# k^T v of a linear-attention block: the last 64 positions as products of 64 rows, and another written-out order of the steps

## The chip, the cores and the metric

The kernel runs on one core of a Trainium2 chip. The metric is the device time of one execution, in microseconds (us); the median of several executions is compared. [...]

## The reference

Eight batches, eight heads, 576 positions, head size 64. What must be computed, for each batch:

```python
q_s = softmax(q, over the head's 64 channels)
k_s = softmax(k, over the 576 positions)
x   = q_s @ (k_s^T @ v)                  # per head, heads side by side: (576, 512)
h   = gelu(x @ w_in)                     # (576, 1024); u, v = halves of 512 columns
v_n = layer_norm(v) * g_ln
out = x + (u * (w_sg @ v_n + b_sg)) @ w_out
```

The results are wanted in float32. The large products are made from float32 numbers that are split in a high and a low part (three products for one); the products of the attention are taken in plain float32, and each of those shows as two matmul instructions in the trace.

## The kernel before

Everything is written out: `PLAN` is a text of 1199 steps such as `hu_mm 3 1`, each a function with its arguments (batch first), and the kernel calls them in that order. Each engine issues its own instructions in that order (`InOrder`, and `keep_in_program_order` for matmuls); the letters V, A and G at the end of a step put it on VectorE (DVE), ScalarE (ACT) or GpSimd (POOL). All transfers are issued by SyncE, in the order of the plan too.

The steps of one batch `b`: `load_k`, `load_v`, `load_q` for each half `h` of the heads (four heads in a half); `k_sub`, `k_exp` (softmax of k without its sum; the column maxima come through `load_kt`, `kt_max`, `kt_put`, `kt_get`); `kv_mm b h`, which makes k^T v and, by a column of ones in v, the sums; `kv_inv` and `kv_scale` divide; `q_max` to `q_mul` make the softmax of q and `q_turn` transposes it; `x_mm b h` makes x; `x_high` and `x_low` split it. Then the block of the MLP: `hv_mm b i` (v half, with `hv_gelu`, `hv_stat`, `hv_pow`, `hv_norm`, `hv_high`, `hv_low`), `hu_mm b f` (u half, with `hu_gelu`), `sg_mm`, `gate`, `gate_high`, `gate_low`, `out_mm`, `out_add`, `out_rest`, `out_store`. Four pieces of 128 columns make one matrix; positions are 4 x 128 and a rest of 64, and the rests of two batches share one `hv_mm b 4`.

Sums lie in PSUM: `ps2` has three buffers of two banks (for `x`, `hu_mm`, `sg_mm`, `out_mm`), `ps1` two buffers of one bank (`kv_mm`, `hv_mm`), each taken in turn.

Batch 0 and the weights are the start. `load_q0` to `q0_copy` prepare q of batch 0, `k0_max`, `k0_mm`, `k0_exp`, `k0_less`, `k0_copy` its k, which is turned on TensorE (`k0_mm b p both` also adds the negated maxima by a second product). `load_w_in f`, `wi_a`, `wi_b`, `wi_d` rebuild a float32 piece of w_in from words in three passes (ACT, DVE, DVE), `wi_h` makes the high part and `wi_l` the low part; pieces 4 and 6 are pairs of 256 columns, so of twice the size. Pieces 0 to 3 are for `hu0_mm f j s` (batch 0's u half, in parts), 4 to 7 for `hv_mm`. Before any data has come, `busy(ps1[0], 21)` issues 21 products of ones, which are not used.

Before, `kv_mm b h` puts the products of one half of the heads in one bank. The fifth block of 128 rows holds the last 64 positions; its other 64 rows of v are zeros.

Of the kernel before, what the change touches and what calls it, by code (L numbers as in the profile page):

```python
# [38 lines left out]
kv_mm 0 1, load_w_in 1, load_w_in 2, q0_turn 0 0, q0_copy 0 1, wi_a 1, wi_b 3, wi_d 3, kv_inv 0 1, q0_copy 0 0, k0_mm 0 0, load_v 0 0, q0_mul 1 1
q0_turn 1 1, k0_mm 0 1, k0_copy 0 0, wi_b 1, load_w_in 0, kv_scale 0 1, wi_a 2, k0_copy 0 1, x0_mm 1 0, wi_h 3 G, q0_copy 1 1, wi_d 1, wi_h 1 G  # L40
kv_mm 0 0, wi_l 3 V, wi_b 2, x0_high 1 0, wi_d 2, neg, load_q 1 0, wi_l 1 V, x0_mm 1 1, kv_inv 0 0, wi_a 0, kv_scale 0 0, load_q 1 1, x0_high 1 1
wi_h 2 G, q_max 1 0, load_w_in 6, x0_neg 1 0, x0_mm 0 0, x0_low 1 0 A, x0_high 0 0, q_max 1 1, x0_neg 1 1, wi_l 2, x0_low 1 1 A, load_w_in 7
# [4 lines left out]
hu0_mm 2 0 0, hu0_mm 1 0 0, hu0_gelu 1 1, hu0_mm 2 1 0, hu0_gelu 2 0, load_w_out 1, hu0_gelu 2 1, hu0_mm 3 0 0, hu0_gelu 3 0, hv_mm 0 3, load_w_out 0
k0_max 1 2, q_sum 1 0, load_kt 2 0, q_swapd 1 0 G, hu0_gelu 1 0, hv_mm 0 0, k0_less 1 1, load_w_sg 0, q_sum 1 1, k0_less 1 0, q_swapd 1 1 G, k0_mm 1 0
k0_less 1 3, k0_less 1 2, q_inv 1 0, q_mul 1 0 1, q_mul 1 0 0, q_inv 1 1, q_turn 1 1, q_mul 1 1 1, k0_mm 1 1, k0_mm 1 2, hv_gelu 0 3, q_turn 1 0
k0_copy 1 1, wo_a 2, wo_b 2, hv_gelu 0 0 A, k0_copy 1 0, hv_mm 0 2, hv_gelu 0 2 A, q_turn 1 3, k0_mm 1 3, k0_copy 1 2, k0_copy 1 3, load_w_sg 1  # L50
kv_mm 1 0, kv_inv 1 0, kv_scale 1 0, wo_a 0, wo_d 2, load_kt 2 1, kv_mm 1 1, kv_inv 1 1, x_mm 1 0, wo_b 0, wo_d 0, hv_sq 0 0, kv_scale 1 1
hu0_mm 0 0 1, hu0_mm 0 0 0, q_mul 1 1 0, q_turn 1 2, load_w_sg 3, hv_mm 0 1, ws_h 0, ws_l 0, load_w_sg 2, x_high 1 0, x_low 1 0, x_high 1 1, x_low 1 1
x_mm 1 1, hv_sq 0 2, hv_gelu 0 1, hv_stat 0 3, hu0_mm 0 1 1, hv_norm 0 3, hv_norm 0 0, hv_stat 0 0 A, hv_pow 0 0, load_v 2 0, hv_stat 0 2 A
x_high 1 3, load_w_sg 4, x_high 1 2, hv_pow 0 2, x_low 1 2, hu0_mm 0 1 0, x_low 1 3, hv_high 0 0, hv_low 0 0, hv_pow 0 3, hv_high 0 3, hv_norm 0 2
hv_low 0 3, kt_max 2 1, load_q 2 0, kt_max 2 0, ws_h 2, ws_l 2 V, hv_stat 0 1, hv_norm 0 1, hv_high 0 2, hv_mm 0 4, hv_gelu 0 4 A, hv_sq 0 4
hv_pow 0 1, hv_mm 1 2, hv_gelu 1 2 A, hv_low 0 2, ws_h 4, load_b, load_v 2 1, hv_stat 0 4 A, hv_pow 0 4, wo_h 2, hv_mm 1 3, b_h, hv_gelu 1 3
hv_high 0 1, q_max 2 0, hv_norm 0 4, wo_h 0 V, load_kt 2 3, kt_max 2 3, load_kt 2 2, hv_mm 1 1, kt_max 2 2, hv_low 0 1, hv_mm 1 0, load_q 2 1
tail_high 0, tail_again 0, ws_l 4 V, hu0_gelu 0 0, tail_high 1, load_k 2 0, hu0_gelu 0 1, q_swapm 2 0 G, hv_stat 1 3, tail_low 0, b_l, sg_mm 0 0
hv_gelu 1 1 A, hv_sq 1 1, hv_norm 1 1, gate 0 0, load_kt 3 0, gate_high 0 0, q_max 2 1, q_swapm 2 1, hv_pow 1 3, sg_mm 0 1, kt_put 2, kt_get 2
load_k 2 1, wo_l 2 V, hv_sq 1 2, gate_low 0 0, gate 0 1, kt_max 3 0, gate_high 0 1, sg_mm 0 2, gate 0 2, gate_high 0 2, wo_l 0, sg_mm 0 3  # L60
tail_again 1, gate_low 0 1, k_sub 2 0, gate_low 0 2 G, gate 0 3, gate_high 0 3, gate_low 0 3, k_sub 2 1, out_mm 0 2, tail_low 1, k_exp 2 0, k_exp 2 1
q_top 2 0, q_sub 2 0 V, out_mm 0 1, hv_stat 1 1 A, q_top 2 1, q_sub 2 1 V, hv_norm 1 3, out_add 0 2, out_add 0 1, q_exp 2 1, q_exp 2 0, load_kt 3 1
q_sum 2 0, hv_gelu 1 0 A, hv_sq 1 0, hv_stat 1 2 A, hu_mm 1 0, q_sum 2 1, hv_pow 1 2, hv_norm 1 2, hv_high 1 2, q_swapd 2 1 G, kt_max 3 1
hv_stat 1 0 A, q_swapd 2 0 G, q_inv 2 0, q_mul 2 0 0, load_kt 3 3, q_turn 2 0, hv_pow 1 0, out_mm 0 3, hu_gelu 1 0, out_add 0 3, hv_norm 1 0
q_mul 2 0 1, out_rest 0 2 V, hu_mm 1 2, hv_high 1 0, hv_low 1 0, kt_max 3 3, out_mm 0 0, hv_pow 1 1, kv_mm 2 0, load_k 3 0, kv_mm 2 1, hv_high 1 3
kv_inv 2 0, hu_gelu 1 2, out_add 0 0, hu_mm 1 3, hu_gelu 1 3, q_turn 2 1, load_q 3 0, out_rest 0 0 V, kv_scale 2 0, kv_inv 2 1, kv_scale 2 1
hv_low 1 2, hv_high 1 1, hv_low 1 1, q_inv 2 1, q_mul 2 1 1 V, load_kt 3 2, q_turn 2 3, hv_low 1 3, q_mul 2 1 0 V, q_max 3 0, q_swapm 3 0 G, hu_mm 1 1
kt_max 3 2, sg_mm 1 0, q_top 3 0, q_turn 2 2, gate 1 0, q_sub 3 0, hu_gelu 1 1, sg_mm 1 1, gate 1 1, gate_high 1 1, sg_mm 1 2, gate 1 2, x_mm 2 0
gate_high 1 0, gate_low 1 0 G, x_high 2 1, out_rest 0 1 V, out_rest 0 3, x_high 2 0, x_low 2 1, gate_low 1 1, gate_high 1 2, sg_mm 1 3, x_low 2 0
gate 1 3, q_exp 3 0, gate_high 1 3, x_mm 2 1, q_sum 3 0, q_swapd 3 0, x_high 2 2, x_high 2 3, gate_low 1 2 G, gate_low 1 3, q_inv 3 0, x_low 2 2  # L70
x_low 2 3, load_q 3 1, q_mul 3 0 1, out_store 0 2, out_mm 1 2, out_add 1 2, q_max 3 1, hv_mm 2 0, load_k 3 1, hv_gelu 2 0, hv_stat 2 0, hv_norm 2 0
q_swapm 3 1, q_top 3 1, q_sub 3 1 V, q_exp 3 1, hv_pow 2 0, hv_high 2 0, q_sum 3 1, out_mm 1 1, hv_mm 2 1, hv_gelu 2 1 A, out_store 0 1, q_mul 3 0 0
kt_put 3, kt_get 3, k_sub 3 1, out_mm 1 3, k_sub 3 0, q_swapd 3 1 G, out_add 1 1, out_rest 1 1 V, q_inv 3 1, out_store 0 0, q_mul 3 1 1 V, out_mm 1 0
out_add 1 0, hv_sq 2 1, load_v 3 1, load_v 3 0, q_turn 3 1, out_rest 1 0, hu_mm 2 2, q_turn 3 0, k_exp 3 0, kv_mm 3 0, out_store 0 3, out_add 1 3
out_rest 1 3 V, kv_inv 3 0, kv_scale 3 0, k_exp 3 1, kv_mm 3 1, q_mul 3 1 0, kv_inv 3 1, x_mm 3 0, out_rest 1 2 V, load_kt 4 0, hv_stat 2 1 A
load_v 4 0, x_high 3 1, hv_mm 2 2, x_high 3 0, out_store 1 1, q_turn 3 2, kv_scale 3 1, hu_gelu 2 2, x_low 3 1, q_turn 3 3, hv_norm 2 1, x_low 3 0
hv_low 2 0, hv_mm 2 3, x_mm 3 1, hv_gelu 2 3 A, hv_sq 2 3, hu_mm 2 0, hv_gelu 2 2 A, x_high 3 2, x_low 3 2, x_high 3 3, x_low 3 3, load_q 4 1
out_store 1 0, out_store 1 3, hv_mm 2 4, hv_sq 2 2, hv_stat 2 2 A, hv_gelu 2 4, hv_stat 2 3 A, q_max 4 1, q_swapm 4 1 G, kt_max 4 0, hu_gelu 2 0
# [843 lines left out]
```

## Time and profile before

| | |
|---|---|
| median of 3 executions | 496.68 us (495.06 to 497.91) |
| the profiled execution, its own time | 495.04 us |
| its span, first to last instruction | 493.3 us |
| TensorE busy in the span | 486.4 us (99%) |
| VectorE, ScalarE, GpSimd busy | 336.3, 239.0, 153.1 us |

A row of the trace gives the start in us from the span's start, the duration, the engine, the line of the code (a helper's, here always L241 for matmuls and L154 for the other engines), the operation, and what it writes and reads by the names of the tiles. Matmuls overlap in the array, so the distance between two starts tells more than one duration does.

### The profile page before, as it was taken

The page shows a single profiled execution, that of the slowest core. Times are in us where ns is not written, and L with a number is a line of the kernel's source. Part 1 is how long each engine was busy: PE and PEld are TensorE (multiplying, and loading weights), DVE is VectorE, ACT ScalarE, POOL GpSimd, SP SyncE. Part 2 cuts the span into 40 slices and gives each one's busy share as a digit, 9 for nine tenths or more (in the row PEclk, how much of TensorE's full clock was granted, in tenths as well). Part 3 has the DMA queues.
Part 4 walks back from the last instruction along what each step waited for, and adds up shares of the span by engine and source line. Part 5 has one row for each costly group of instructions (what it writes and reads, how often), then busy time and mean ns, then how long its engine had stood idle before and what let it go on. Part 6 is the DMA issues. An engine that isn't in the chain of part 4 may idle for free.

```text
span 493.3 us, 9408 instructions
## 1 busy us (share of the span) xinstructions
PE 486.4 (99%) x3881; PEld 448.3 (91%) x3881; DVE 336.3 (68%) x550; ACT 239.0 (48%) x402; POOL 153.1 (31%) x189
## 2 busy tenths in 40 slices
PE   7999999999999999999999999999999999999997
...
DVE  7998997877679576787575577785659753353232
...
PEclk9999999999999999999999999999999999999999
...
GB/s 306 360 389 246 176 175 76 25 79 101 182 143 78 206 125 88 49 177 251 2 155 22 63 219 47 25 102 154 45 256 25 24 76 0 1 0 2 96 1 96
DMA packets 20637, 57.28 MB, mean 116 GB/s; under 512 B 3057, under 2 KB 3569, under 8 KB 20594
## 3 DMA queue, kind: packets, MB, share of 16 engines
...
## 4 chain that ended last, share of the span: by engine, by line
PE 94%; DVE 3%; DMA 2%; issue 1%; ACT 0%; SPq 0%
PE ps L241 94%; DMA qq<-q 2%; DVE o L154 1%; DVE wi_l L154 1%; DVE qd L154 0%; DVE k0m L154 0%; ACT o L154 0%; DVE qm L154 0%; DVE qq L154 0%; SPq L154 0%
## 5 line engine op out<-in xcount | busy, mean ns | idle before, releaser
L241 PE MATMUL ps<-ulow,wo_h 128*128 128x288 f32 (+1 forms) x260 | 56.6, 295 | 0.0
L241 PE MATMUL ps<-gh,wo_h 128*128 128x288 f32 (+1 forms) x260 | 56.5, 295 | 0.0
L241 PE MATMUL ps<-gh,wo_l 128*128 128x288 f32 (+1 forms) x260 | 56.4, 294 | 0.0
L154 DVE TENSOR_TENSOR u<-ps,u 128x576 f32<-128x576 f32 x32 | 23.9, 754 | 46.1 <-PE ps L241 45.9
L241 PE MATMUL ps<-ws_h,vnh 128*128 128x288 f32 x256 | 55.1, 296 | 0.0
L241 PE MATMUL ps<-ws_l,vnh 128*128 128x288 f32 x256 | 54.8, 295 | 0.0
L241 PE MATMUL ps<-ws_h,vnl 128*128 128x288 f32 x256 | 54.8, 295 | 0.0
L154 POOL TENSOR_TENSOR rs<-ve,half 128x1 f32<-128x1 f32 x36 | 26.8, 752 | 90.1 <-DVE ve L154 90.0
L154 ACT CAST gh<-u 128x576 fp32r<-128x576 f32 x32 | 21.1, 670 | 58.2 <-DVE u L154 58.2
L154 ACT ACT_TABLE_LOAD x32 | 41.1, 1283 | 14.5 <-issue 3.5
L154 ACT ACTIVATE u<-ps 128x576 f32<-128x576 f32 (+2 forms) x36 | 21.0, 596 | 50.6 <-PE ps L241 42.1
L241 PE MATMUL ps<-x_h,wi_h 128*128 128x288 f32 (+2 forms) x256 | 42.4, 300 | 1.0 <-ACT u L154 1.0
L241 PEld LDWEIGHTS ps<-gh,wo_h 128*128 128x128 f32 x260 | 42.2, 188 | 0.8 <-issue 0.4
L241 PEld LDWEIGHTS ps<-ws_h,vnh 128*128 128x128 f32 x256 | 41.6, 188 | 1.4 <-DVE u L154 0.9
L154 POOL TENSOR_TENSOR ulow<-u,gh 128x576 fp32r<-128x576 f32 x15 | 24.0, 1598 | 60.5 <-ACT gh L154 50.7
L241 PEld LDWEIGHTS ps<-gh,wo_l 128*128 128x128 f32 x260 | 42.2, 188 | 0.0
L241 PEld LDWEIGHTS ps<-ulow,wo_h 128*128 128x128 f32 x260 | 42.0, 188 | 0.1
L241 PEld LDWEIGHTS ps<-x_h,wi_h 128*128 128x128 f32 x256 | 36.5, 188 | 5.4 <-issue 2.6
L241 PEld LDWEIGHTS ps<-ws_h,vnl 128*128 128x128 f32 x256 | 41.3, 188 | 0.0
L241 PEld LDWEIGHTS ps<-ws_l,vnh 128*128 128x128 f32 x256 | 41.3, 188 | 0.0
L241 PE MATMUL ps<-x_h,wi_l 128*128 128x288 f32 (+2 forms) x256 | 41.3, 296 | 0.0
L241 PE MATMUL ps<-x_l,wi_h 128*128 128x288 f32 (+2 forms) x256 | 41.2, 295 | 0.0
...
## 6 DMA issues: line engine op xcount, KB each, us to landing
...
```

The lines of the kernel that those rows point to most:

```text
L154: ins = op(*args, **kw)
L241: tc.keep_in_program_order(nc.tensor.matmul(*args, **kw))
```

## The change

The new kernel has `kv_all b` in place of the two `kv_mm b h` for batches 2 to 7. It makes the four full blocks of rows for both halves of the heads first, and then the last 64 positions as products of 64 rows: head pair `a = 0` uses the upper 64 rows of the array and of the data, `a = 1` the lower ones, so v now holds the last positions in both halves of its fifth block. The sums of `a` lie in the bank of `a`, with both `h` in it, which turns the places in `kvt` (`kv_of`). Batches 0 and 1 keep `kv_mm`.

`k0_mm 0 3` is the first product with data (before, `k0_mm 0 2`) and gets four more products of ones after its first transposition.

The order of nearly all steps is another one, and many steps change engine: the high parts of w_in go from POOL to DVE (`wi_h` 1, 0, 6) and ACT (2, 3, 4), four of the low parts from DVE to POOL (`wi_l` 1, 0, 3, 4) and `wi_l 2` from POOL to DVE; `q0_sub 1 1` and `k0_copy 0 0` go to DVE; six of twelve `k_sub` go from DVE to POOL. No step other than `kv_mm` and `kv_all` is added or removed.

```diff
     def k0_mm(b, p, both=0, n=0):
         ps, t = flat(bank(ps2, "k0", b, p)), kt0(b, p)
-        busy(ps[:, 0:DV], n)
         for i in range(5):
             c = min(i * P, S - P)
             mm(ps[:, i * P:i * P + P], t[:, c:c + P], eye, is_transpose=True, start=True, stop=not both)
+            busy(ps1[0], n * (i == 0))
+    def kv_all(b):
+        for a in range(2):
+            bank(ps1, "kv", b, a)
+        pk = [sums(st["kv", b, a]) for a in range(2)]
+        for h in range(2):
+            for a in range(2):
+                for i in range(4):
+                    for z in range(2):
+                        c = a * P + z * D
+                        mm(pk[a][z * D:z * D + D, h, :], kk_s(b, h)[:, i, c:c + D], vv_s(b, h)[:, i, 2 * a + z, :], start=h == i == 0, stop=False, skip_group_check=h == 1)
+        for h in range(2):
+            for a in range(2):
+                for z in range(2):
+                    c, rs = a * P + z * D, slice(a * TL, a * TL + TL)
+                    mm(pk[a][z * D:z * D + D, h, :], kk_s(b, h)[rs, 4, c:c + D], vv_s(b, h)[rs, 4, 2 * a + z, :], start=False, stop=True, skip_group_check=h == 1)
+    def kv_of(b, h, a):
+        return kvt_s(b, a)[:, h] if b > 1 else kvt_s(b, h)[:, a]
# in x_mm:      kvt_s(b, h)[zs, a]  ->  kv_of(b, h, a)[zs]
# in kernel():
-    vs[:2, S:] = vs[:2, ST * P:S]
+    vs[:, S:] = vs[:, ST * P:S]
# PLAN before, in part:
-load_q0 1 0, q0_max 1 0, q0_sub 1 0, load_q0 0 1, q0_max 0 1, load_q0 1 1, q0_exp 1 0, q0_max 1 1, q0_sum 1 0, q0_sub 0 1, q0_sub 1 1, load_k0 0 3
-load_k0 0 2, q0_exp 0 1, q0_exp 1 1, q0_sum 0 1, q0_inv 1 0, q0_inv 0 1, k0_max 0 2, load_eye, k0_mm 0 2 1, load_q0 0 0, q0_max 0 0, q0_mul 0 1
...
-load_w_out 2, q_exp 1 0, load_k0 1 3, load_k0 1 0, wi_l 0 V, wi_a 4, wi_d 6, hu0_mm 1 0 1, hu0_mm 1 1 1, q_exp 1 1, hu0_mm 1 1 0, wi_h 6 G, load_v 1 1
-wi_b 4, wi_d 4, wi_h 4 G, load_g, k0_max 1 1, hu0_mm 3 1 0, hu0_gelu 3 1, wi_l 6 V, load_w_out 3, wi_l 4 V, k0_max 1 3, k0_max 1 0, load_v 1 0
# PLAN after, in part:
+load_q0 0 0, q0_max 0 0, q0_sub 0 0, q0_exp 0 0, load_q0 1 1, q0_max 1 1, load_q0 1 0, q0_sub 1 1 V, q0_exp 1 1, q0_max 1 0, q0_sub 1 0, q0_sum 1 1
+load_q0 0 1, q0_max 0 1, q0_exp 1 0, load_k0 0 3, load_eye, q0_inv 1 1, q0_sub 0 1, load_k0 0 2, load_w_in 2, q0_exp 0 1, k0_max 0 3, k0_mm 0 3 1 4
...
+kv_mm 0 0, load_w_in 6, wi_l 0, wi_l 3, x0_neg 1 0, x0_neg 1 1, kv_inv 0 0, kv_scale 0 0, x0_low 1 0 A, q_max 1 0, x0_mm 0 0, x0_low 1 1 A, x0_mm 0 1
+x0_high 0 0, x0_neg 0 0, load_w_in 7, q_max 1 1, x0_high 0 1, q_swapm 1 0 G, x0_low 0 0 A, load_w_in 4, x0_neg 0 1, q_top 1 0, q_sub 1 0 V
+x0_low 0 1 A, load_w_in 5, load_k0 1 1, load_w_out 1, q_swapm 1 1, hu0_mm 2 0 1, hu0_mm 2 1 1, hu0_mm 2 0 0, hu0_mm 2 1 0, q_top 1 1, wi_a 6
+load_k0 1 2, hu0_mm 3 0 1, hu0_mm 3 1 1, load_k0 1 0, hu0_mm 1 0 1, q_exp 1 0, q_sub 1 1 V, q_exp 1 1, load_k0 1 3, hu0_mm 3 1 0, load_w_out 0, wi_b 6
+hu0_mm 1 1 1, wi_d 6, load_w_out 3, wi_h 6 V, hu0_mm 1 1 0, hu0_mm 1 0 0, wi_a 4, wi_b 4, hu0_gelu 2 1, hu0_gelu 3 1, wi_d 4, hu0_mm 3 0 0, wi_l 6 V
+load_v 1 1, wi_h 4, wi_l 4, hu0_gelu 2 0, load_v 1 0, k0_max 1 2, hu0_gelu 1 1, hu0_gelu 3 0, q_sum 1 1, hv_mm 0 3, load_w_out 2, k0_max 1 3
...
+q_turn 3 0, q_turn 3 1, out_mm 1 2, out_add 1 2, hu_mm 2 2, hu_gelu 2 2, kv_all 3, kt_max 4 1, q_mul 3 1 1, hu_mm 2 3, q_turn 3 3, kv_inv 3 0
+load_kt 4 3, out_rest 1 2, out_rest 1 3, hu_gelu 2 3, load_v 4 0, kv_scale 3 0, kv_inv 3 1, kv_scale 3 1, load_q 4 0, x_mm 3 0, hv_stat 2 3 A
...
+gate_low 7 3, out_mm 7 0, out_add 7 0, out_store 7 0, out_mm 7 1, out_add 7 1, out_store 7 1, out_mm 7 2, out_add 7 2, last_mm 7 0, both 7 3 V
+out_store 7 2, last_mm 7 2, last_add 7 0, last_add 7 2, last_store 7 0, last_store 7 2, last_mm 7 1, last_add 7 1, last_store 7 1
```

On TensorE, by the plans, the neighbours of these steps change as follows. Before, in batches 3, 5, 6 and 7 the two `kv_mm` are followed directly by `x_mm b 0`; in batches 2 and 4 another product lies between. After, another product (`hu_mm` or `out_mm`) follows `kv_all` in all six. `x_mm b 0` and `x_mm b 1` stand apart in all batches, before and after. In batch 0 the small products stood as three groups (`x0_mm 1 0, kv_mm 0 0, x0_mm 1 1`, then `x0_mm 0 0`, then `x0_mm 0 1`) and stand as two (`x0_mm 1 0, x0_mm 1 1, kv_mm 0 0`, then `x0_mm 0 0, x0_mm 0 1`).

## Rows read from the trace of the kernel before

**Rows 1.** The page: busy time of each engine (share of the span, instructions), and the span in 40 slices with the granted TensorE clock and the DMA engines' share, in tenths.

```profile
PE 486.4 (99%) x3881; PEld 448.3 (91%) x3881; DVE 336.3 (68%) x550; ACT 239.0 (48%) x402; POOL 153.1 (31%) x189
...
PE   7999999999999999999999999999999999999997
...
DVE  7998997877679576787575577785659753353232
...
PEclk9999999999999999999999999999999999999999
```

**Rows 2.** The chain of work that ended last, in order of time (start, us, what); the parts from the first product with data to the end.

```profile
9.49 8.56 PE ps L241 x94
...
18.11 4.91 DMA qq<-q
...
32.94 1.23 DVE o L154
34.17 0.66 DVE k0m L154
34.83 2.67 DVE wi_l L154 x2
37.54 118.88 PE ps L241 x1008
...
156.46 334.02 PE ps L241 x2592
```

**Rows 3.** What TensorE's matmuls waited for in the whole span (us in total, times, longest).

```profile
PE ps L241 <- POOL vn L154: 1.3, 1, 1.3
PE ps L241 <- DVE k0m L154: 1.1, 1, 1.1
PE ps L241 <- ACT u L154: 1.0, 1, 1.0
```

**Rows 4.** The order of time on TensorE around small products (start, duration, x count), in the start and in batches 2 and 3.

```profile
18.66 0.66 PE L241 MATMUL ps<-qt,kvt 64*64 64x256 f32 x8
19.26 1.39 PE L241 MATMUL ps<-vv,kk 128*64 128x65 f32 x40
20.57 0.77 PE L241 MATMUL ps<-qt,kvt 64*64 64x320 f32 x8
21.27 0.50 PE L241 MATMUL ps<-x_h,minus 128*128 128x256 f32 x2
...
105.09 0.43 PE L241 MATMUL ps<-ulow,wo_h 128*128 128x288 f32 x2
105.35 0.43 PE L241 MATMUL ps<-gh,wo_l 128*128 128x288 f32 x2
105.71 2.55 PE L241 MATMUL ps<-vv,kk 128*64 128x65 f32 x80
108.19 0.80 PE L241 MATMUL ps<-x_h,wi_h 128*128 128x288 f32 x4
...
125.98 1.20 PE L241 MATMUL ps<-qt,kvt 64*64 64x288 f32 x16
127.11 0.53 PE L241 MATMUL ps<-ws_h,vnh 128*128 128x288 f32 x2
```

**Rows 5.** Busy time of the engines in one stretch of the start (us; stretch, its length, then PE, PEld, DVE, ACT, POOL, granted clock, DMA share, GB/s).

```profile
3.40:32.00 28.60, 27.13 (x256) 22.30 (x256) 26.10 (x48) 22.32 (x36) 14.13 (x17) 1.00 1.00 374
```

**Rows 6.** The order of time on TensorE at the end of the start: the last `hu0_mm`, and `hv_mm 0 3` (rows of `wi_h,x_h`, `wi_h,x_l`, `wi_l,x_h`).

```profile
32.73 0.46 PE L241 MATMUL ps<-x_l,wi_h 128*128 128x320 f32 x2
34.19 0.50 PE L241 MATMUL ps<-x_h,wi_h 128*128 128x256 f32 x2 [1.01 <-ACT u L154]
...
34.77 0.40 PE L241 MATMUL ps<-x_l,wi_h 128*128 128x256 f32 x2
35.33 1.21 PE L241 MATMUL ps<-wi_h,x_h 128*128 128x512 f32 x4 [0.17 <-POOL wi_h L154]
36.38 1.09 PE L241 MATMUL ps<-wi_h,x_l 128*128 128x512 f32 x4
37.54 1.20 PE L241 MATMUL ps<-wi_l,x_h 128*128 128x512 f32 x4
```

**Rows 7.** Groups of instructions by operation and shape (busy us in all, mean ns of one): the steps that change engine, and their nearest kin on the engine they go to.

```profile
L154 DVE TENSOR_TENSOR wi_l<-o,wi_h 128x512 fp32r<-128x512 f32 x3 | 2.0, 682 | 0.0
L154 DVE CAST wo_h<-o 128x1024 fp32r<-128x1024 f32 x1 | 0.7, 685 | 0.0
L154 DVE TENSOR_TENSOR qq<-qq,qd 128x512 f32<-128x512 f32 x1 | 0.7, 693 | 0.0
L154 DVE TENSOR_TENSOR o<-ps,o 128x576 f32<-128x576 f32 x3 | 2.3, 758 | 5.8 <-PE ps L241 5.8
...
L154 POOL CAST wi_h<-o 128x1024 fp32r<-128x1024 f32 x2 | 2.1, 1046 | 5.5 <-DVE o L154 5.5
L154 POOL TENSOR_TENSOR wo_l<-o,wo_h 128x1024 fp32r<-128x1024 f32 x1 | 2.7, 2661 | 0.0
...
L154 ACT CAST wo_h<-o 128x1024 fp32r<-128x1024 f32 x1 | 1.1, 1053 | 0.0
```

**Rows 8.** The order of time on VectorE in the start (start, duration; in brackets the idle time before it and what ended it).

```profile
4.44 0.82 DVE L154 TENSOR_REDUCE qm<-qq 128x10 f32<-128x640 f32 x1 [0.27 <-DMA qq<-q]
6.03 0.82 DVE L154 TENSOR_REDUCE qm<-qq 128x10 f32<-128x640 f32 x1 [0.77 <-DMA qq<-q]
...
8.74 0.69 DVE L154 TENSOR_REDUCE k0m<-ukt 128x1 f32<-128x576 f32 x1
...
20.69 0.16 DVE L154 TENSOR_SCALAR kr<-ps 128x2 f32<-128x2 f32 x1 [0.26 <-PE ps L241]
...
23.04 1.35 DVE L154 TENSOR_REDUCE qm<-qq 128x36 f32<-128x1152 f32 x1 [0.41 <-DMA qq<-q]
```

**Rows 9.** Groups as in rows 7: what VectorE and POOL have between `kv_all 3` and `x_mm 3 0` in the new order.

```profile
L154 DVE STREAM_TRANSPOSE qt<-qq 128x576 f32<-128x576 f32 x28 | 21.1, 766 | 4.5 <-POOL qq L154 4.4
...
L154 DVE TENSOR_TENSOR kvt<-ps,kr 128x128 f32<-128x128 f32 x16 | 4.6, 285 | 0.3
...
L154 DVE RECIPROCAL kr<-kr 128x2 f32<-128x2 f32 x16 | 2.7, 166 | 0.5
...
L154 POOL TENSOR_TENSOR qq<-qq,qd 128x576 f32<-128x576 f32 x19 | 24.4, 1294 | 7.4 <-ACT x_h L154 3.8 <-DVE qd L154 2.6 <-DVE qm L154 0.9
```

**Rows 10.** The order of time on VectorE at the end of the span: the last `last_add`.

```profile
490.51 0.31 DVE L154 TENSOR_TENSOR o<-ps,o 128x144 f32<-128x144 f32 x1 [0.84 <-PE ps L241]
```

More of the change, by code (lines that the diff above doesn't have):

```diff
@@ L39 @@
[L39 to L42, printed above, removed]
@@ L47 @@
[L47 to L50, printed above, removed]
@@ L51 @@
[L51 to L78, printed above, removed]
@@ L99 @@
-out_add 3 2, load_kt 6 1, out_rest 3 2, out_add 3 1, q_mul 5 1 1, kv_inv 5 0, hv_stat 4 0 A, kv_scale 5 0, q_mul 5 1 0, q_turn 5 2, hv_norm 4 0
-kv_mm 5 1, kv_inv 5 1, out_rest 3 1 V, out_store 3 1, x_mm 5 0, x_high 5 0, hv_high 4 3, out_store 3 0, hv_mm 4 2, x_high 5 1, x_low 5 1, kv_scale 5 1
-hv_gelu 4 2 A, hv_low 4 3, hv_sq 4 2, hv_pow 4 0, q_turn 5 3, load_q 6 1, x_low 5 0, hu_mm 4 1, load_k 6 0, x_mm 5 1, hu_gelu 4 1, x_high 5 2
-x_low 5 2, kt_max 6 2, hv_high 4 0, hu_mm 4 3, load_k 6 1, q_max 6 1, x_high 5 3, x_low 5 3, hv_mm 4 4, q_max 6 0, hv_gelu 4 4 A, hv_sq 4 4
@@ new lines @@
+k0_less 0 0, q0_mul 1 1, q0_mul 0 0, k0_max 0 1, k0_exp 0 2, q0_sum 1 0, q0_turn 1 1, q0_turn 0 0, q0_copy 0 0, q0_inv 1 0, wi_b 2, q0_mul 1 0 V
+wi_d 2, q0_mul 0 1, load_w_in 1, wi_a 1, load_w_in 3, q0_copy 1 1, load_w_in 0, wi_b 1, wi_d 1, wi_h 1 V, q0_turn 0 1, k0_less 0 1, kv_mm 0 1
+kv_inv 0 1, load_v 0 0, q0_copy 0 1, q0_turn 1 0, q0_copy 1 0, k0_mm 0 0, k0_copy 0 0 V, kv_scale 0 1, wi_l 1, wi_h 2, k0_mm 0 1, wi_l 2 V, wi_a 0
+wi_b 0, x0_mm 1 0, x0_mm 1 1, wi_a 3, load_q 1 0, k0_copy 0 1, x0_high 1 1, wi_b 3, wi_d 0, wi_d 3, x0_high 1 0, wi_h 3, load_q 1 1, wi_h 0 V
@@ new lines @@
+q_mul 1 1 1 V, hu0_gelu 1 0, q_turn 1 3, wo_a 0, hv_mm 0 2, hv_stat 0 3, k0_copy 1 1, q_turn 1 0, q_mul 1 0 1, q_turn 1 1, hv_gelu 0 2 A, q_mul 1 1 0
+wo_b 0, k0_mm 1 2, wo_d 0, k0_mm 1 3, load_kt 2 0, kv_mm 1 0, kv_inv 1 0, k0_copy 1 2, k0_copy 1 3, kv_mm 1 1, kv_scale 1 0, x_mm 1 0, kv_inv 1 1
+kt_max 2 1, load_kt 2 3, load_w_sg 3, wo_a 2, kv_scale 1 1, hv_sq 0 0, wo_b 2, wo_d 2, hu0_mm 0 0 1, ws_h 0, ws_l 0, hv_pow 0 3, q_turn 1 2
+load_v 2 1, hu0_mm 0 0 0, x_high 1 1, x_high 1 0, hv_sq 0 2, x_low 1 0, x_low 1 1, hv_stat 0 2 A, hv_mm 0 1, kt_max 2 3, load_kt 3 0, x_mm 1 1
```

141 lines of the change are left out of this document (82 added, 59 removed).

## The prediction

> **What bounds the kernel now.** I read the page first. TensorE is busy for 99% of the span at the full clock in every slice; only the first and the last slice are below nine tenths, while VectorE is at nine tenths in most of the first slices and then falls [rows 1]. So the end is set by TensorE's work, and by what keeps it from working in the start.
>
> The chain says where that is [rows 2]: TensorE from 9.49, then a load of q, then in the main VectorE (the rows at 32.94, 34.17 and 34.83 are its), and from 37.54 TensorE alone, in two pieces of 118.88 and 334.02 us, to the end. The waits agree [rows 3]: in the whole span TensorE's matmuls wait for another engine three times by more than 0.3 us, and all three lie before 36 us. The reader is to see that after the start there is nothing to win by a better order: 453 us of products stand back to back. A new order can only save waits of the start, or switches of TensorE between kinds of products; and it can add waits anywhere.
>
> **k^T v, product by product.** Two products of 288 columns take 0.26 to the next start (105.09 to 105.35), so one 0.13. Going over to the run of 80 small ones takes 0.36 in place of 0.26, so leaving the full array costs 0.10; after the return the first two products last 0.53 where two last 0.43, so returning costs 0.10 [rows 4]. A run of 80 takes 2.48 up to the next start, a run of 40 takes 1.31: 0.0585 for two instructions (they start together in the two column halves), and 0.14 fixed for each run. An `x_mm` works in quarters of the array, four instructions at a time: its 4 rounds of 288 columns take 1.13; 2 rounds of 256 take 0.60 and of 320 0.70, so 2 rounds of 288 some 0.65; a round is 0.24, and 0.17 is fixed [rows 4].
>
> The trace has no products of 64 rows and 65 columns. By proportion a round of 65 columns costs 0.24 x 65 / 288 = 0.054. `kv_all` is then 32 pairs, 32 x 0.0585 + 0.14 = 2.01, and 4 rounds with their switch, 4 x 0.054 + 0.17 = 0.39: 2.40 against 2.48, or 0.08 saved in a batch and 0.5 in six. Bounds: if the switch inside is free, 1.0 more is saved; if the four do not run together, the tail is 8 pairs, 0.47 + 0.17 = 0.64, and `kv_all` 2.65, 1.0 lost in six. I take the value by the rounds, since the quarters are those of `x_mm`.
>
> But the neighbours change. In batches 3, 5, 6 and 7 the small products were one run with `x_mm b 0`, and now a full product lies between. Each split costs one more way out and back, 0.20, in four batches 0.8. Together: -0.5 + 0.8 = **+0.3 us**. The half-rows give less than the order takes back.
>
> In batch 0 three groups of small products become two, worth some 0.5 by the same prices. I count it as nothing, because TensorE waits at the end of this stage anyway: the cover is the wait for `hv_mm 0 3`, 1.6 us below. Without that cover it is a gain of 0.5.
>
> **The start.** `hv_mm 0 3` starts at 35.33; the product before it ends its turn so that without waits it could start at about 33.7 (32.73 + 0.29 for the two rows of 320, then 0.70 for the six of 256: 0.58 from 34.19 to 34.77 without the switch's 0.10, and 0.23 for the last two) [rows 6]. What it waits for is VectorE's rebuilding of w_in (`wi_b 4`, `wi_d 4`, which ends at 34.17) and then `wi_h 4` [rows 2]. VectorE's queue therefore sets the start, and it is nearly full: from 3.4 to 32 us it is idle for 2.5 of 28.6 us [rows 5], of which four waits make 1.7 [rows 8].
>
> The new order puts ahead of `wi_d 4` on VectorE: `q0_sub 1 1` (0.693 x 640/512 = 0.87), `k0_copy 0 0` (0.758 x 640/576 = 0.84), `wi_l 2` (0.68), `wi_h 1` and `0` (half of 0.685 each) and `wi_h 6` (0.685): 3.8. It takes away `wi_l 3`, `1` and `0`, 3 x 0.682 = 2.05 [rows 7]. Net +1.7 of work, against 1.7 of waits which it may fill: the chain ends between 0 and 1.7 later. The first added step lies in the 0.77 gap of rows 8, but `k0_copy 0 0` now makes VectorE wait for TensorE's `k0_mm 0 0` with `kv_scale 0 1` behind it, for which `x0_mm 1 0` waits. I take +0.5. `wi_h 4` costs the same on ScalarE (1.05) as on POOL (1.05) [rows 7]; it stands behind a `hu0_gelu`, which is over before `wi_d 4` ends.
>
> `wi_l 4` goes to POOL, where the like piece of w_out takes 2.66 [rows 7]. The first eight products of `hv_mm 0 3` need only the high part and last 1.05 + 0.93 = 1.98; before, the ninth then waited 0.23 (37.54 against 35.33 + 1.98) [rows 6]. Now it waits about 0.7: **+0.45**. Start together **+1.0**.
>
> The first product with data stays where it is. On VectorE seven steps on q lie ahead of `k0_max 0 3` (four maxima, a difference, a sum, an inversion), as seven lie ahead of `k0_max 0 2` now (three maxima, two sums, two inversions): a maximum and a difference of some 0.7 to 0.9 for a sum and an inversion, with two waits to absorb it. I leave its end where `k0_max 0 2` ends, at 9.4 (8.74 + 0.69) [rows 8]. The four products of ones at 0.23 each fit in TensorE's wait of 1.1 before it [rows 3]; were that wait gone, they would cost 0.9.
>
> On SyncE's queue the loads of w_in 4 to 7 stand behind `load_q 1 1`, which waits until q of batch 0 has been turned out of its buffer. Now that is at 18.05, and q lands 4.91 later [rows 2], 0.41 late for VectorE [rows 8]. In the new order it waits for `q0_turn 1 0`, which is the last `q0_turn` too, with one `k0_mm` more behind it than now. The bytes ahead are the same pieces in another order, so I put it at the same time; a delay of up to 1 us would meet `q_max 1 1` behind more work on VectorE than now.
>
> Costed at nothing: `k_sub` on POOL, the two more table loads of ScalarE that the order asks for, and all moves on POOL. POOL is busy for 31% and ScalarE for 48% [rows 1]; the cover is one or more products of 3 us between maker and user. The tail keeps its form, three parts with one of 144 columns last [rows 10].
>
> **Sum.** +0.3 + 1.0 = +1.3 us. On the profiled execution (495.04) this is 496.3; on the median (496.68), 498.0. The executions of one kernel lie 2.9 us apart, so I take the middle of the two: **497.2 us**. Half a per cent, 2.5 us, is about what a measurement of this kernel can tell from no change.
>
> **Rivals.** Times are from the same middle, 495.9. (1) Faster: POOL takes over four of the low parts, and the 2.05 that VectorE loses counts in full, because all its added steps fall into its waits. Then TensorE is the bound, `hv_mm 0 3` starts when it can, 1.6 earlier, and the groups joined in batch 0 give 0.5: -2.1 + 0.3 = -1.8, 494.1. For it: the four waits. Against: 3.8 of added work for 1.7 of waits. 0.15.
>
> (2) Slower: `x_mm b 0` now needs the scalings of both halves, and `kv_all` delivers both only at its end. In batch 3 one `hu_mm` (24 products, 3.2 us) lies between; VectorE has there `kt_max` (0.69 as the reduction of rows 8), `q_turn` 0.77 and twice the three steps of the scaling (0.29, 0.17 and a third as short, 0.6 in all), together 2.7, and `q_turn` waits for a `q_mul` of 1.29 on POOL [rows 8, 9]. Once POOL is late by over 0.5, TensorE waits. At 1 us in three of six batches this is +3: 500.2. Against: the old order has no such wait after 38 us. 0.20.
>
> (3) The 64-row products do not run together. Then `kv_all` is 2.65 and the six batches cost 1.5 more than forecast: 498.7. The rows speak against it: the loads and products of `x_mm` start four at a time. 0.10. [...]
>
> **Numbers.** The forecast has 0.55. Slower by over 0.5% comes from (2) and a little of (3) and of the forecast's own spread: 0.23. Faster by over 0.5% comes from (1), which ends close to the bound: 0.10. The rest, 0.67, is the same. The range runs from (1) to just past (2): 493.9 to 500.6.
>
> **What would show it.** Right: `kv_all` 2.4 us with 16 of its instructions in rounds of four; a full product behind each; `hv_mm 0 3` near 35.8 to 36.3 with a wait for POOL's `wi_l` inside; no wait over 0.3 us after 45 us. Wrong: `hv_mm 0 3` before 35, waits of TensorE for VectorE's `kvt`, or a run of `kv_all` over 2.6.

## The result and the profile after

The new kernel takes 499.11 us (median of 7 runs, 498.93 to 500.19), the kernel before beside it 496.68 (495.06 to 497.91): ratio 1.0058, 95% interval 1.0039 to 1.0078, so 0.6% slower. The predicted time was 497.2 and the range went to 500.6. The profiled execution of the new kernel is the longest of its seven, 500.19 us with a span of 498.4; the other six have spans of 497.2 to 497.9, and a mean granted clock of 0.997 where it has 0.993. So the profile shows the case at its worst.

The page, as in [rows 1]:

```profile
PE 490.1 (98%) x3885; PEld 451.4 (91%) x3885; DVE 321.1 (64%) x537; ACT 245.1 (49%) x421; POOL 173.6 (35%) x185
...
PE   8999999999999999999999999997999999999997
...
PEclk9999999999999999999999999997999999999999
```

In [rows 1] nothing between the first and the last slice was below nine tenths. Now one slice is, two thirds of the way through the span, and its clock is low too. What TensorE waited for, as in [rows 3] (us in total, times, longest):

```profile
PE ps L240 <- DVE o L153: 2.9, 1, 2.9
PE ps L240 <- POOL vn L153: 1.3, 1, 1.3
PE ps L240 <- ACT o L153: 0.7, 1, 0.7
PE ps L240 <- POOL wi_l L153: 0.3, 1, 0.3
```

The first line is new; it is the only wait after 45 us that this view lists, and what the new kernel loses lies there: one wait of 2.9 us. The windows around it (stretch, length, then busy time with counts of PE, PEld, DVE, ACT, POOL, granted clock, DMA share, GB/s):

```profile
337.00:340.20 3.20, 0.33 (x3) 0.10 (x1) 1.45 (x3) 0.00 (x0) 0.00 (x0) 0.89 0.53 205
340.20:346.20 6.00, 5.97 (x25) 5.97 (x26) 3.24 (x7) 0.65 (x1) 0.00 (x0) 0.50 0.01 3
346.20:352.00 5.80, 5.80 (x45) 5.80 (x45) 3.18 (x4) 0.68 (x1) 1.88 (x1) 0.99 0.13 51
```

TensorE stands still for 2.9 us, and then works for 6 us at a granted clock of 0.50, before it is back at 0.99 (third row). In those 6 us it starts 25 products; a version without the wait (experiment 2) starts 47 in the same stretch. 25 / 47 x 6.0 = 3.2, so the low clock costs another 2.8. In this execution a wait of 2.9 us has cost 5.7. In the other six it cost less: a mean clock of 0.997 over 497 us is, by estimate, 1.5 us lost to the clock, and the medians below agree with that.

The chain through that place, in order of time (start, us, what; SPq is SyncE issuing a load):

```profile
333.95 0.33 SPq L153
...
334.37 0.38 SPq L153
...
334.80 4.64 DMA kmt<-kt
339.44 0.75 DVE o L153
...
340.23 1.81 PE ps L240 x6
```

and VectorE's queue there:

```profile
338.75 0.75 DVE L153 TENSOR_REDUCE ktall<-kmt 128x1 f32<-128x576 f32 x1 [3.38 <-DMA kmt<-kt]
339.43 0.75 DVE L153 TENSOR_TENSOR o<-ps,x_h 128x576 f32<-128x576 f32 x1
```

SyncE is idle until 333.95, when `kv_all 6` ends and `load_k 7 0` gets its buffer. Behind `load_k 7 0`, in the same queue, stands `load_kt 7 2`, which needs nothing from `kv_all 6`; it is issued at 334.37 and has landed 4.4 later, at 338.75, when VectorE, idle for 3.38, reduces it in `kt_max 7 2`. (The 4.64 us from 334.80 in the chain are those of the next load in the queue, `load_kt 7 3`; it lands as `out_add` begins, and the chain puts `out_add` down to it. What `out_add` stands behind on VectorE is `kt_max`, which experiment 1 shows.) Behind `kt_max` stands `out_add 4 3`, whose data had been there since about 328, when the product behind `out_mm 4 3` began. `out_mm 4 1` needs the PSUM bank that `out_add 4 3` empties. One load is late by the place it has in a queue, and four engines stand: VectorE is idle for 3.38 until it has landed, and from 337.00 to 340.20 TensorE is busy for 0.33, ScalarE and POOL for 0.00.

At the start the new kernel gains. The end of the start on TensorE, as in [rows 6]:

```profile
34.10 0.40 PE L240 MATMUL ps<-x_l,wi_h 128*128 128x256 f32 x2
34.34 1.09 PE L240 MATMUL ps<-wi_h,x_h 128*128 128x512 f32 x4
35.27 1.07 PE L240 MATMUL ps<-wi_h,x_l 128*128 128x512 f32 x4
36.61 1.20 PE L240 MATMUL ps<-wi_l,x_h 128*128 128x512 f32 x4 [0.27 <-POOL wi_l L153]
```

`hv_mm 0 3` starts at 34.34 without a wait, against 35.33 before. By `kv_mm 1 0` (45.52 against 46.47) the new kernel is 0.95 ahead. This is its earliest start: in seven other traces with the new order throughout (below) `hv_mm 0 3` starts at 34.48 to 34.88 and `kv_mm 1 0` at 45.69 to 46.07.

The sum of the two profiled executions: spans 498.4 - 493.3 = 5.1; -0.95 start, +2.9 wait, +2.8 low clock leaves 0.35 for everything else; 0.2 of it is what the new order takes longer from `kv_mm 1 0` on where nothing waits (see k^T v, below).

### The profile page after: what moved, and what is told of

Same layout as the page of the kernel before. It is cut to its first block, busy times and chain, and to the rows that moved or that the text cites. A ratio compares the mean times of both kernels' runs of the same rounds, so it can differ in the third digit from the quotient of the medians.

```text
span 498.4 us, 9402 instructions
## 1 busy us (share of the span) xinstructions
PE 490.1 (98%) x3885; PEld 451.4 (91%) x3885; DVE 321.1 (64%) x537; ACT 245.1 (49%) x421; POOL 173.6 (35%) x185
## 4 chain that ended last, share of the span: by engine, by line
PE 94%; DMA 2%; ACT 2%; POOL 1%; issue 0%; SPq 0%; DVE 0%; POOLq 0%
PE ps L240 94%; DMA raw_x_h<-w_out 1%; DMA kmt<-kt 1%; POOL wi_l L153 0%; ACT o L153 0%; ACT qt L153 0%; ACT wi_h L153 0%; ACT L153 0%; ACT qq L153 0%; SPq L153 0%; DVE o L153 0%; ACT u L153 0%; ACT ukt L153 0%; POOL vn L153 0%; POOLq L153 0%
## 5 line engine op out<-in xcount | busy, mean ns | idle before, releaser
L240 PE MATMUL ps<-gh,wo_h 128*128 128x288 f32 (+1 forms) x260 | 58.0, 301 | 2.9 <-DVE o L153 2.9
L240 PE MATMUL ps<-ulow,wo_h 128*128 128x288 f32 (+1 forms) x260 | 57.8, 301 | 0.0
L153 POOL TENSOR_TENSOR rs<-ve,half 128x1 f32<-128x1 f32 x36 | 24.1, 673 | 86.9 <-DVE ve L153 86.7
L153 ACT ACTIVATE v<-ps 128x512 f32<-128x512 f32 x36 | 21.6, 600 | 46.9 <-PE ps L240 42.8
L240 PEld LDWEIGHTS ps<-gh,wo_l 128*128 128x128 f32 x260 | 43.3, 193 | 0.0
L240 PEld LDWEIGHTS ps<-ulow,wo_h 128*128 128x128 f32 x260 | 43.1, 193 | 0.1
```

Source lines behind the costliest of these rows:

```text
L153: ins = op(*args, **kw)
L240: tc.keep_in_program_order(nc.tensor.matmul(*args, **kw))
```

## The experiments

Each ran beside the kernel before on its chip; ratios are to that, with 95% intervals.

**1. `kt_max 7 2` behind `out_add`.** One step of the new kernel is moved.

```
-... load_kt 7 2, kt_max 7 2, out_add 4 3, out_mm 4 2, ... hv_low 5 2, out_add 4 2, out_rest 4 2 V
+... load_kt 7 2, out_add 4 3, out_mm 4 2, ... hv_low 5 2, out_add 4 2, kt_max 7 2, out_rest 4 2 V
```

> The new kernel with one step moved: kt_max 7 2 stands behind out_add 4 2 in VectorE's queue instead of ahead of out_add 4 3. Theory (a queue behind a load): load_k 7 0 may only be issued when kv_all 6 has read the old k; load_kt 7 2 stands behind it on SyncE, kt_max 7 2 waits for that load on VectorE, out_add 4 3 stands behind kt_max 7 2, and TensorE waits 2.9 us for out_add 4 3 and then works at the lower clock. Then the wait and the lower clock both go: span 492.5 to 493.5, median 494.8 to 495.6. Rival (out_add 4 3 is late for another reason, or the work behind it only moves the wait to the next bank): TensorE still waits over 1 us near 337, median 497.5 or more.

Measured: 495.44 us (494.96 to 496.08, 12 runs), ratio 0.9974 [0.9953, 0.9996]. The wait for `DVE o` and the low clock are gone; a smaller wait of TensorE remains near the same place, behind a smaller wait of VectorE:

```profile
339.26 0.75 DVE L152 TENSOR_REDUCE ktall<-kmt 128x1 f32<-128x576 f32 x1 [0.58 <-DMA kmt<-kt]
```
```profile
341.99 0.54 PE L239 MATMUL ps<-ws_h,vnl 128*128 128x288 f32 x2 [0.65 <-DVE vnl L152]
```

It is `kt_max` again, now ahead of `hv_low 5 0`. So the 3.7 us between the medians of the two versions (0.8% by their ratios to the kernel before) hang on the place of one reduction of 0.75 us. They fit 2.9 of wait and some 1.5 of clock, less the 0.65 that remain.

**2. The load earlier.** `kt_max 7 2` keeps its place; its load goes ahead of the load that waits.

```
-... gate_low 4 3, load_k 7 0, q_inv 6 1, ... hv_high 5 0, load_kt 7 2, kt_max 7 2, out_add 4 3
+... gate_low 4 3, load_kt 7 2, load_k 7 0, q_inv 6 1, ... hv_high 5 0, kt_max 7 2, out_add 4 3
```

> The new kernel with one step moved: load_kt 7 2 stands ahead of load_k 7 0 on SyncE; kt_max 7 2 stays ahead of out_add 4 3 on VectorE. Theory A (the load stood behind one that waits for kv_all 6 to give its buffer free): it is issued by 331, lands some 4.6 later, before kt_max's turn; TensorE's wait of 2.9 at 337 and the low clock after it are gone, 495.0 to 496.5 us, no TensorE wait over 1 us after 45 us. Rival B (VectorE's queue is late by itself, the load only ends its last wait): out_add 4 3 still comes late by over 1 us, 498 or more.

Measured: 494.54 us (494.41 to 494.97, 7 runs), ratio 0.9945 [0.9922, 0.9969]. SyncE's queue and VectorE in that stretch:

```profile
321.59 0.43 SPq L152 DMA_DIRECT2D kmt<-kt  x1
334.33 0.33 SPq L152 DMA_DIRECT2D kk<-k  x1
```
```profile
335.69 0.74 DVE L152 TENSOR_REDUCE ktall<-kmt 128x1 f32<-128x576 f32 x1
```

The load goes out at 321.59, 12.7 us ahead of `load_k 7 0`, and `kt_max` runs at 335.69 with no idle time before it. The window that had the low clock:

```profile
340.20:346.20 6.00, 6.00 (x47) 6.00 (x46) 3.23 (x5) 0.66 (x1) 1.87 (x1) 1.00 0.14 52
```

Theory A holds, and below its range: this removes the remaining wait of experiment 1 as well. After the start the view of waits has no line for TensorE any more. By its ratio this version beats both kernels, but how far it beats the kernel before depends on which executions of that one stand beside it (experiment 9): here 12 of 14 were long ones. Against the short ones, under 496 us, it is only 0.3 faster (two of them here), and 0.6 on the chip of experiment 5 (twelve of them).

**3. Both.** The load ahead, and `kt_max 7 2` behind `hv_low 5 0` too.

> The new kernel with load_kt 7 2 ahead of load_k 7 0 and kt_max 7 2 behind hv_low 5 0 on VectorE. If what is lost in batch 6 is VectorE's queue there and nothing else: no wait of TensorE over 0.3 us between 300 and 400 us, 494.5 to 495.4 us, 0.3 to 0.7 below the version with only kt_max moved (495.44). If another wait takes its place: 495.4 or more, and the trace names it.

Measured: 494.74 us (494.29 to 494.91, 6 runs), ratio 0.9944 [0.9923, 0.9966]. The same as with the load alone, on the same chip (494.54): nothing was left in VectorE's queue there, and the expectation that it would come out below the first version was met by the load, not by the place of `kt_max`.

**4. The old products in the new order.** Each `kv_all b` becomes `kv_mm b 0, kv_mm b 1`, as before the change.

```
-... kv_all 6, kv_inv 6 1, kv_scale 6 1, ...
+... kv_mm 6 0, kv_mm 6 1, kv_inv 6 1, kv_scale 6 1, ...
```

> The new kernel in its new order, with the pair kv_mm b 0, kv_mm b 1 of the kernel before in place of each kv_all b (and v with zeros again). Theory: the products cost 0.08 us more per batch (+0.5 in six), and the k buffer of half 0 is free about 1.2 us earlier, so that load_k 7 0 and load_kt 7 2 land 1.2 us earlier and the wait near 337 shrinks from 2.9 to about 1.7 with less time at the lower clock: median 497.5 to 498.8. Rival (the half-row products are what costs the time): median 496.5 or less, with the wait gone. Rival (the wait has nothing to do with when kv_all ends): 499.5, wait 2.9.

Measured: 497.26 us (496.67 to 498.67, 12 runs), ratio 1.0027 [1.0007, 1.0046]. The wait in batch 6 is there, 1.8 in place of 2.9, and in the profiled execution the clock behind it keeps its level (two of the twelve, 498.53 and 498.67, have a mean of 0.997):

```profile
337.80:342.00 4.20, 2.42 (x18) 2.19 (x17) 3.54 (x6) 0.65 (x1) 0.00 (x0) 1.00 0.14 56
342.00:348.00 6.00, 6.00 (x48) 6.00 (x47) 3.37 (x8) 0.01 (x1) 1.87 (x1) 1.00 0.14 52
```

`kv_mm 6 0` gives half of k free before `kv_all 6` would: `load_k 7 0` goes out at 333.68 here and at 333.95 in the new kernel, though that is 0.4 ahead by `kv_mm 1 0`. So the wait belongs to the order, and the product form adds about 1 us to it; in the new kernel the clock falls behind it. The time is a little under what was expected, and in ten of twelve executions the clock held. Because of the wait, this run doesn't price the products. The next one does.

**5. The price of the products alone.** The version of experiment 2, once with the old products and once as it is, on one chip.

> The version with load_kt 7 2 ahead of load_k 7 0, with the products of k^T v done as before (each kv_all b as kv_mm b 0 and kv_mm b 1, 80 products against weights of 128 rows and zeros for the missing 64). Theory A (a kv_all is 0.08 cheaper than the pair, nothing else): six times 0.08 = 0.5 above the version with kv_all of the same call, 494.9 to 495.3 where that has 494.5. Rival B (earlier sums from kv_mm b 0 save a wait that kv_all makes): no longer than the version with kv_all, 494.5 or less.

> The version with load_kt 7 2 ahead of load_k 7 0 a second time, beside the run above on the same chip: 494.4 to 494.8, as the first time.

Measured: 495.19 us (494.81 to 495.54, 10 runs) with the old products, 494.69 (494.46 to 494.97, 10 runs) with `kv_all`; neither has a wait after the start. 0.50 in six batches, 0.08 in one, as forecast; from `kv_mm 1 0` to the end their traces differ by 0.5 too (447.5 and 447.0). Rival B falls.

**6. The new products in the old order.** The order before, with each pair `kv_mm b 0`, `kv_mm b 1` drawn together into `kv_all b` at the place of the second, and the scalings behind it.

> The order of the kernel before with kv_all b in place of each pair of kv_mm; the scalings that stood ahead of it or behind x_mm b 0 are moved to the place they need, as close as possible. Products alone: -0.08 us in each of six batches, -0.5, median 496.2. But in batches 3, 5, 6 and 7 x_mm b 0 follows kv_all directly and needs both scalings, which start when kv_all ends: two times 0.15 + 0.17 + 0.29 with 0.05 between, about 1.3 us of wait in each of the four, +5 together: median 500 to 502. If the wait is hidden, 496 to 497.

Measured: 508.32 us (506.26 to 510.86, 6 runs), ratio 1.0248 [1.0211, 1.0284]. TensorE's first line of waits, one of the places (batch 5), and the window behind it:

```profile
PE ps L239 <- DVE kvt L152: 6.3, 6, 1.8
```
```profile
281.57 0.69 PE L239 MATMUL ps<-qt,kvt 64*64 64x288 f32 x2 [1.69 <-DVE kvt L152]
282.69 2.19 PE L239 MATMUL ps<-qt,kvt 64*64 64x288 f32 x14 [0.43 <-DVE kvt L152]
```
```profile
282.00:288.00 6.00, 5.57 (x24) 3.30 (x23) 1.68 (x5) 3.08 (x6) 0.00 (x0) 0.52 0.28 101
```

This is the mechanism of rival 2 of the prediction: `x_mm b 0` needs both scalings, these need the whole `kv_all`, and with no other product between, TensorE waits, six times, 6.3 us together, all in batches 3, 5, 6 and 7. In batches 2 and 4, where this order has another product between, it doesn't wait. Behind the waits of batch 5 its clock is at 0.52 (the window), and the six executions have means of 0.987 to 0.993. The loss is greater than I expected: I priced the waits, at some 5, and not the clock. (The profiled execution, at 510.86 the longest of the six, also lost 3.0 in its start: `kv_mm 1 0` at 49.47.) So `kv_all` needs an order that splits it from `x_mm` by a full product.

**7. The new start alone.** The new order as far as `hv_mm 0 0`, then the remaining steps of the order before, with the old products.

> The new order up to and with hv_mm 0 0 (with the four more products of ones), then the remaining steps in the order and on the engines of the kernel before, with kv_mm. Theory: the start of the new order is 0.95 us shorter (kv_mm 1 0 starts at 45.53 instead of 46.48 in the two traces) and nothing gives it back, since TensorE is full from there on: median 495.4 to 496.0. Rival (the gain of the start is lost again in the waits that follow, as buffers come free when they did): 496.5 or more.

Measured: 497.10 us (496.52 to 497.25, 12 runs), ratio 1.0008 [0.9986, 1.0031]. `hv_mm 0 3` starts at 34.41, as early as in the new kernel, but `kv_mm 1 0` only at 47.71. Two waits lie between:

```profile
41.58 1.86 PE L239 MATMUL ps<-eye,kk 128*128 128x128 f32 x15 [0.86 <-ACT kk L152]
44.15 1.21 PE L239 MATMUL ps<-wi_h,x_h 128*128 128x512 f32 x4 [0.72 <-ACT v L152]
```

ScalarE is busy without a gap there, with four table loads (`ACT_TABLE_LOAD` in the trace, 1.28 each), 5.1 us between 35 and 43.5, where the new kernel has two between 34.9 and 40.3. My expectation failed: here a start that was ahead on TensorE was worth nothing, since what follows asks the exponentials and the GELUs of ScalarE in the old sequence. That the two more table loads are what makes ScalarE late is read from the trace; no run takes them out alone.

**8. POOL's cast and VectorE.** The new kernel rounds the high part of w_in piece 6 (`wi_h 6`) on VectorE, the kernel before on POOL, where it runs beside `wi_b 4` on VectorE. The two are exchanged, one in each kernel. In the new kernel:

```
-... load_w_out 3, wi_h 6 V, hu0_mm 1 1 0, ...
+... load_w_out 3, wi_h 6 G, hu0_mm 1 1 0, ...
```

> The new kernel with wi_h 6 (a cast of 128x1024) on POOL in place of VectorE. Theory A (VectorE's steps of this kind stand still while POOL's cast runs): the step wi_b 4 that then runs beside the cast takes about 1.5 us instead of 0.69, so that taking 0.69 of work off VectorE brings nothing: wi_d 4 ends at 32.9 to 33.1 as in the new kernel and hv_mm 0 3 starts at 34.2 to 34.5. Rival B (no such effect; the 1.54 in the kernel before has another cause): wi_b 4 stays at 0.69, wi_d 4 ends at 32.2 to 32.4.

In the kernel before:

```
-... hu0_mm 1 1 0, wi_h 6 G, load_v 1 1, wi_b 4, ...
+... hu0_mm 1 1 0, wi_h 6 V, load_v 1 1, wi_b 4, ...
```

> The kernel before with wi_h 6 on VectorE in place of POOL. Theory A (POOL's cast holds VectorE up): wi_b 4 falls from 1.54 to about 0.69, so that the 0.69 added to VectorE costs nothing: wi_d 4 ends at 33.9 to 34.1 against 34.17, and hv_mm 0 3 starts no later than 35.35. Rival B: wi_b 4 stays at 1.5, wi_d 4 ends at 34.8 to 34.9 and hv_mm 0 3 starts at 36.0.

Measured by the step, in order: `wi_b 4` and POOL's cast of the kernel before, `wi_b 4` of the new kernel, then the first exchange (VectorE, POOL), then the second:

```profile
31.36 1.54 DVE L154 TENSOR_SCALAR o<-o 128x1024 uint32<-128x1024 uint32 x1
```
```profile
31.31 1.04 POOL L154 CAST wi_h<-o 128x1024 fp32r<-128x1024 f32 x1 [3.62 <-DVE o L154]
```
```profile
30.97 0.69 DVE L153 TENSOR_SCALAR o<-o 128x1024 uint32<-128x1024 uint32 x1
```
```profile
31.16 1.04 DVE L152 TENSOR_SCALAR o<-o 128x1024 uint32<-128x1024 uint32 x1 [0.69 <-ACT o L152]
```
```profile
30.61 1.04 POOL L152 CAST wi_h<-o 128x1024 fp32r<-128x1024 f32 x1 [5.12 <-DVE o L152]
```
```profile
33.30 0.69 DVE L152 CAST wi_h<-o 128x1024 fp32r<-128x1024 f32 x1
33.91 0.69 DVE L152 TENSOR_SCALAR o<-o 128x1024 uint32<-128x1024 uint32 x1
```

With the cast on VectorE the step takes 0.69 in either kernel; beside POOL's cast 1.54 or 1.04, with 0.99 or 0.49 of the cast left when the step begins. In the second exchange the stretch from the start of `wi_d 6` to the end of `wi_d 4` is 32.06 to 35.86 = 3.80, against 30.04 to 34.17 = 4.13 before: VectorE does 0.69 more work in 0.33 less time. The absolute times of that run (497.93, one execution) missed the expectation (`hv_mm 0 3` at 37.02, not 35.35), because a load of q landed some 2 us late; that is experiment 9. The first exchange (499.57, one execution) showed a smaller effect on `wi_b 4` than expected, since the step had to wait 0.69 for ScalarE first and met only the second half of the cast. Its `wi_d 4` ends at 33.46 and `hv_mm 0 3` starts at 34.70, both 0.2 to 0.4 later than theory A had; in the traces that leave the cast on VectorE they come at 32.92 to 33.48 and 34.34 to 34.88. So taking 0.69 of work off VectorE brought nothing, and rival B (`wi_d 4` by 32.4) falls. This run has the wait in batch 6 too, 3.0 us, and loses less clock than the new kernel's profile: its mean clock over the execution is 0.997 against 0.993.

**9. The kernel before, twice more.** The executions of the kernel before spread over 5 us. Of 63 timed beside these experiments 27 are under 496 us and 31 over 497, with 5 between; the profiled one (495.04) is of the lower group.

> The kernel before, unchanged, profiled a second time. Its executions lie in two groups, near 494.8 at a granted clock of 0.999 to 1.0 and near 497.7 at 0.995 to 0.997; the profiled one of the prediction belongs to the first. Theory A (the load of q for batch 1 lands late in the second group): in a trace of the second group VectorE waits about 2 us for DMA qq at 23 to 25, TensorE then waits 2 us or more before hv_mm 0 3, and its clock is at 0.5 for some us behind that wait; in a trace of the first group none of it. Rival B: the second group loses its time elsewhere, after 45 us, with the start as in the first trace.

> The same kernel a third time, for a second sample of the two groups: the same expectation by group as for the run before it.

Measured: 497.58 and 495.53 us, one of each group. VectorE's wait for q, TensorE's wait that comes of it, and the clock behind it, in the long execution:

```profile
24.42 1.35 DVE L154 TENSOR_REDUCE qm<-qq 128x36 f32<-128x1152 f32 x1 [1.64 <-DMA qq<-q]
```
```profile
PE ps L241 <- ACT u L154: 2.2, 1, 2.2
```
```profile
38.00:39.00 1.00, 1.00 (x3) 0.72 (x3) 1.00 (x2) 0.99 (x2) 0.00 (x0) 0.50 1.02 410
```

and in the short one:

```profile
23.64 1.35 DVE L154 TENSOR_REDUCE qm<-qq 128x36 f32<-128x1152 f32 x1 [0.25 <-DMA qq<-q]
```
```profile
PE ps L241 <- ACT u L154: 0.8, 1, 0.8
```
```profile
38.00:39.00 1.00, 0.92 (x5) 0.76 (x5) 1.00 (x3) 0.50 (x1) 0.00 (x0) 1.00 1.01 414
```

Theory A holds for these two: q lands 1.6 us late instead of 0.25 (0.41 in [rows 8]), TensorE waits 2.2 instead of 0.8, and the clock falls to 0.50 for some 3.5 us (0.81, 0.50, 0.50, 0.50 and 0.98 in the five windows of 1 us from 36). From `kv_mm 1 0` to the end the two executions and the first trace are alike to 0.1 us (446.8). Experiment 6 and the second exchange of experiment 8, which have the old start, show the same wait of TensorE in their traces, 2.2 and 2.1. The late q needn't account for all of the upper group: five of its 31 executions have a mean clock of 1.000, and none of those was profiled. Why the load lands late in one execution and not in another isn't settled. In the new order the loads of q go out earlier, at 15.45 (first row) against 16.57 (second, the kernel before), and none of its traces shows TensorE waiting there.

```profile
15.45 2.18 SPq L153 DMA_DIRECT2D qq<-q  x2
```
```profile
16.57 1.86 SPq L154 DMA_DIRECT2D qq<-q  x2
```

## Why the prediction was right or wrong

**The number** was 1.9 us under the median and inside the range, and it was luck: two errors of opposite sign. The start came out 2 us better than its term (-0.95 for +1.0), and a wait that no term held took more than that back, some 4.4 us in most executions with the clock behind it. Of the prediction's own signs, "`hv_mm 0 3` before 35" was one of being wrong, and it came; "no wait over 0.3 us after 45 us" was one of being right, and it failed.

**k^T v: right.** `kv_all` was forecast at 2.40. The new trace (batch 3, start and duration, then the two shapes with their counts and mean ns):

```profile
107.83 2.48 PE L240 MATMUL ps<-vv,kk 128*64 128x65 f32 x80
110.23 0.93 PE L240 MATMUL ps<-x_h,wi_h 128*128 128x288 f32 x5
```
```profile
L240 PE MATMUL ps<-vv,kk 128*64 128x65 f32 x64 | 2.1, 223 | 0.0
L240 PE MATMUL ps<-vv,kk 64*64 64x65 f32 x16 | 0.5, 230 | 0.0
```

110.23 - 107.83 = 2.40. The sixteen products of 64 rows start in rounds of four, the second round 0.108 behind the first and the others 0.058 apart, where the proportion to `x_mm` gave 0.054. Rival 3 falls: the four loads of a round start 0.007 apart and last 0.13 each, so they overlap, and the sum by the rows was the right one. Rounds of 64-row loads are 0.058 apart, as are pairs of 128-row loads in the same trace. From `kv_mm 1 0` to the end, without any wait, the old kernel takes 446.8, the version of experiment 2 takes 447.0 to 447.1 and with the old products 447.5: +0.2 and +0.7, where the terms were +0.3 (-0.5 + 0.8) and +0.8. The +0.8 for splitting four batches wasn't run by itself; these two differences agree with it.

**The start: wrong sign.** The step that failed is "net +1.7 of work, against 1.7 of waits", from which I took +0.5 for `hv_mm 0 3`; it came 1.0 earlier (0.5 to 0.9 in the other traces of the new order). I took the durations of VectorE's steps from the trace of before as the price of the work. Three of them hold time in which VectorE stood beside a cast on POOL: `wi_b 4` (1.54 against 0.69), a `q_sub` (1.81 against 1.36), and the four 128x512 steps of w_in (522 ns in the mean against 409): 0.85 + 0.45 + 0.45 = 1.75. The new order takes those casts off POOL, so VectorE gives up 1.75 of standing still for the 1.7 of added work. And its idle time from 3.4 to 32 us fell from 2.5 to 1.6:

```profile
3.40:32.00 28.60, 27.50 (x255) 22.75 (x255) 27.02 (x52) 23.98 (x38) 11.45 (x13) 1.00 1.01 380
```

1.7 - 1.75 - 0.9 makes -0.95, against a measured -1.25 at the end of `wi_d 4` (34.17 to 32.92); the other 0.3 stays open. Of the 1.75 experiment 8 tests the part of `wi_b 4`; the rest is read from durations alone. The slow-down could be seen in the old trace: two steps `o<-o` of 128x1024 on VectorE, one of 0.68 and one of 1.54. I had used only means. What in the chip holds VectorE beside a cast no run shows; the rows show by how much, with 0.69 to 1.54 as the largest case. I didn't look for it, since the change put work *on* POOL in other places; what counted was what it took off. The wait for POOL's `wi_l 4` was priced at 0.45 more and is 0.27, against 0.23 before. The first products with the maxima of k start at 9.32 (9.49 before; I had left them there), and the four products of ones lie before them, from 8.22, at no cost.

**Rival 1 was the mechanism of the start**: TensorE is the bound there, and `hv_mm 0 3` starts when it can, though at 34.34 and not the 33.7 of the estimate. That experiment 2 (494.54) comes near its 494.1 is partly chance, since `hv_mm 0 3` came 1.0 earlier and not 1.6. I had given it 0.15 for the work against it, which was counted in prices that were too high.

**"No wait over 0.3 us after 45 us": wrong**, and it decided the case. Under rivals I looked for waits where a dependency changes (`x_mm` behind `kv_all`), and of SyncE's queue I followed only the start. The first part says that a new order "can add waits anywhere"; the step that failed is that the sum put this at nothing for batches 2 to 7 without following the loads that changed places in SyncE's queue there. `kv_all` frees k only at its end, and what stands behind `load_k` in SyncE's queue is late with it. By experiment 4 the order brings 1.8 us of that wait and `kv_all` the rest. Rival 2 had the right family (a wait after 45 us) with the wrong place; in the new order `kvt` is never waited for, and experiment 6 shows it is the order that prevents it.

**The clock: missed.** No term of the sum held it. A wait of 2.9 us cost 5.7 in the profiled execution and, by estimate from the mean clock, some 4.4 in the other six; in the profiled execution of experiment 4 only the wait of 1.8 itself was lost.

**The base.** I took a middle between the profiled execution and the median as if the spread were noise. It is two groups. The changed start also takes away the late q of the upper group, which costs 2.0 to 2.5 us there (`kv_mm 1 0` at 48.98 against 47.01 and 46.47 in the two short executions); that gain was not in the forecast, and the wait in batch 6 spent it. On SyncE in the start I had put q's loads "at the same time"; they go out 1.1 earlier.
